# Stores of two gradient tiles moved from SyncE to ScalarE, and SyncE's order of transposing loads and late stores fixed by edges

## The chip, the cores and the metric

The kernel runs on one core of one Trainium2 chip. The metric is the device time of one execution in microseconds (us); before the change it is 480.02 us, the median of three runs (479.32 to 480.20). One further execution was taken with the hardware profiler; all durations below come from that one. Five engines work in parallel, each through its own instruction list in order: TensorE (PE, with its weight loads listed as PEld), VectorE (DVE), ScalarE (ACT), GpSimd (POOL) and SyncE (SP), which here does nothing but issue DMA transfers.

## The reference

A forward function and its gradients for a given `grad_out`, with S = 2048 positions, D = 512 channels and F = 1376 hidden units, all in bf16:

```python
def _A_ref(q, k, v, shift_k, ssm_k, ssm_D):
    ...
    for t in range(ks):                                  # a causal shift filter of 4 taps
        k_shift = k_shift + k_pad[:, t:t + S, :] * shift_k[:, ks - 1 - t][None, None, :]
    kv = k_shift * v
    ...
    y = irfft(rfft(kv) * rfft(ssm_k))[:S]                # a causal convolution over 2048 positions
    y = y + kv * ssm_D[None, None, :]
    return q * y
...
g = x @ w_gate; u = x @ w_up                             # x is the normalised A_q
B = (g * u) @ w_down
out = A_q + _A_ref(layernorm(A_q), ...) + B
_out, _vjp = jax.vjp(_f, A_q, A_k, A_v, A_shift_k, A_ssm_k, A_ssm_D, B_w_gate, B_w_up, B_w_down)
```

The outputs are `out` (out_0) and nine gradients: of A_q (out_1), A_k (out_2), A_v (out_3), the shift filter (out_4), ssm_k (out_5), ssm_D (out_6), w_gate (out_7), w_up (out_8) and w_down (out_9).

## The kernel before

The positions are split into 8 chunks of 256, F into 11 blocks `fb` (ten of 128 and a last one of 96). Up to about 316 us the kernel normalises, computes the gate and up projections and the hidden gradients chunk by chunk, and runs the forward and inverse transforms of the convolution in matrix form. Each chunk leaves a tile `hd` with three parts for each F block (the hidden product and the gradients of the two projections); seven of the eight chunks are stored to DRAM as `HDD`, the last one stays on chip.

The change lies in what follows, the part from `dw()` on. `dw()` runs over the 11 F blocks and does for each of them two products over all 16 rows of 128 positions:

- `down_grad(fb)` (L1022 to L1039): 16 matmuls `pd` of 512 columns, whose result ScalarE copies into `od` (two buffers) and SyncE stores into out_9 (L1034). For the last block the two halves of `od` are copied and stored by ScalarE and by VectorE with SyncE (L1036 to L1039).
- the products `pu` (L1062), 64 matmuls, whose result ScalarE copies into `og`; after every odd block, and after the last, SyncE stores `og` in two transfers into out_7 and out_8 (L1073). There is one `og` buffer, shared by two neighbouring blocks.

Both products need the block of the hidden tile with positions on the partitions, so it has to be transposed. For blocks 0 to 6 SyncE loads it as `hb` (L793, two buffers) and TensorE transposes it in `hid_t` (`pt`, L859), from where ScalarE copies it into `nath` and `natd`. For the last four blocks (`TURNED`, 7 to 10) `load_t` (L804 to L820) issues a transposing DMA on SyncE that writes `natT` directly: one load for blocks 7, 8 and 10, two for block 9, five in all. Block 7's takes the buffer of `hb` block 5, block 8's that of `hb` block 6, the others the buffers of earlier `natd` and `nath` tiles. The loads of block fb+2 are written in the middle of `down_grad(fb)`.

Four side generators are woven between the steps of `dw()`; the number n below counts the yields of `dw()`, six to a block:

- `inv_y` from n = 0, every 3rd step: the inverse transform; its VectorE products leave `kb`, stored by SyncE, and `dks`.
- `dsk_gram` from n = 27, every 2nd step: matmuls `pk` and VectorE's products `kd` (L1091) for the shift filter's gradient; TensorE's PSUM pool of three buffers (`p2`) is shared by `pk`, `pt`, `pu` and others.
- `inv_dk` from n = 35: the gradient of ssm_k (`po`, `o5t`).
- `ew` from n = 10, every 3rd step: VectorE's elementwise rounds. It runs the 16 pieces of `tail`: `final(b)` for b = 0 to 7 (out_0 and out_1, tiles `o` and `e`, two buffers each, which read a tile `bb` that `load_fin` loads one round ahead on SyncE, L1127) and `bwd(b)` (out_2, tile `dk`). Their results are put on the list `late`, and `put_late()` (L1178) issues the stores of one piece on SyncE ahead of the next piece.

The list of every engine is ordered when the program is built, by a planner of the framework that goes by its own estimates and by priorities: program order, which `tc.high_priority(offset=SOON)` raises by 300 places. `tc.issue_after(x)` adds an edge: what is traced in its block on the same engine as `x` stands behind `x` in that engine's list. It adds no wait, and nothing at all on another engine. `LG` holds the most recently traced instruction of a kind at the time that the code is traced. Before the change `behind(fb)` gives block 9's transposing loads an edge to the last `bb` load traced, and block 10's an edge to the last `og` store; blocks 7 and 8 have none. The numbering that follows from n: the stores of round 2 (`o`, `e`), `dk` 1 and the load of `bb` 4 are traced ahead of block 7's transposing load; `o`, `e` 3, `dk` 2 and `bb` 5 between block 7's and block 8's; `o`, `e` 4, `dk` 3 and `bb` 6 between block 8's and block 9's; `o`, `e` 5, `dk` 4 and `bb` 7 between block 9's and block 10's.

Of the kernel before, what the change touches and what calls it, by code (L numbers as in the profile page):

```python
# [24 lines left out]
NFB = len(FBLK)  # L25
# [165 lines left out]
def kernel(  # L191
# [24 lines left out]
    nc = tc.nc  # L216
# [14 lines left out]
    def cs(c):  # L231
        return slice(c * 128, (c + 1) * 128)

    def act(o, i):
        nc.scalar.copy(o, i)  # L235
# [7 lines left out]
    BX = dram.tile([P, R, 2, D], BF, name="BX")  # L243
# [8 lines left out]
    def P2(name, shape, dt=F32):  # L252
        return ps2.tile(shape, dt, name=name, tag="p2")

    def P1(name, shape, dt=F32):
        return ps1.tile(shape, dt, name=name, tag="p1")
# [399 lines left out]
    first = ExitStack()  # L656
# [131 lines left out]
    LG = {}  # L788

    def load_hb(fb):  # L790
        f0, fw = FBLK[fb]
        t = CP["b"].tile([P, NCH - 1, 3, 256], BF, name="hb")
        nc.sync.dma_start(t[:fw], HDD[:fw, fb])  # L793
        hbs[fb] = t
# [3 lines left out]
    TURNED = range(NFB - 4, NFB)  # L798

    def behind(fb):  # L800
        first = {NFB - 2: lambda: LG["bb"], NFB - 1: lambda: LG["og"]}.get(fb)
        return tc.issue_after(first().ins) if first else ExitStack()

    def load_t(fb):  # L804

        f0, fw = FBLK[fb]
        if fb == SPLIT:
            parts = ((0, 5, "n", dict(tag="natd", bufs=2)), (5, NCH - 1, "n", dict(tag="nath")))
        elif fw < P:
            parts = ((0, NCH - 1, "n", dict(tag="natd", bufs=2)),)  # L810
        else:
            parts = ((0, NCH - 1, "b", dict(tag="hb")),)
        nats[fb, 0] = {}
        for a, e, pool, kw in parts:
            t = CP[pool].tile([P, e - a, 3, 2, fw], BF, name="natT", **kw)
            with behind(fb) as _, tc.high_priority(offset=SOON):
                nc.sync.dma_start_transpose(out=t[:].rearrange("s c t h f -> s (c t h) f"),
                                            in_=HDD[:fw, fb, a:e].rearrange("p c t s -> p (c t s)"))
            for c in range(a, e):
                nats[fb, 0][c] = t[:, c - a]  # L820
# [3 lines left out]
    def last_t(fb):  # L824
        f0, fw = FBLK[fb]
        pt = P2("pt7", [P, 3, 2, P], BF)
        for t in range(3):
            for h in range(2):
                nc.tensor.transpose(pt[:, t, h, :fw], hds[1][:fw, fb, t, h * 128:h * 128 + 128], ident[:fw, :fw])
        n7 = c2b.tile([P, 3, 2, P], BF, name="nat7", tag="dd")  # L830
        act(n7[:, :, :, :fw], pt[:, :, :, :fw])
        nats[fb, 1] = n7

    def nat_h(fb, r):
        f0, fw = FBLK[fb]
        if fb not in TURNED:
            return nats[fb, 0][:, r, :fw]
        return nats[fb, 0][r // 2][:, 0, r % 2, :] if r < R - 2 else nats[fb, 1][:, 0, r % 2, :fw]

    def nat_d(fb, r):  # L840
        f0, fw = FBLK[fb]
        if fb not in TURNED:
            return nats[fb, 1][:, :, r, :fw]
        return nats[fb, 0][r // 2][:, 1:3, r % 2, :] if r < R - 2 else nats[fb, 1][:, 1:3, r % 2, :fw]

    def hid_t(fb, t):
        if fb in TURNED:
            return
        f0, fw = FBLK[fb]
        hb = hbs.pop(fb) if t == 2 else hbs[fb]  # L850
        if t == 0:
            nats[fb, 0] = CP["n"].tile([P, R, P], BF, name="nath")
        elif t == 1:
            nats[fb, 1] = CP["n"].tile([P, 2, R, P], BF, name="natd", bufs=2)
        dst = nats[fb, 0] if t == 0 else nats[fb, 1][:, t - 1]
        pt = P2("pt", [P, R, P], BF)
        for r in range(R):
            hs = hb[:fw, r // 2, t] if r < R - 2 else hds[1][:fw, fb, t]
            nc.tensor.transpose(pt[:, r, :fw], hs[:, (r % 2) * 128:(r % 2) * 128 + 128], ident[:fw, :fw])  # L859
        act(dst[:, :, :fw], pt[:, :, :fw])  # L860
# [161 lines left out]
    def down_grad(fb):  # L1022
        f0, fw = FBLK[fb]
        pd = P1("pd", [P, D])
        for r in range(R):
            nc.tensor.matmul(pd[:fw, :], lhsT=nat_h(fb, r), rhs=goC[:, r, :], start=(r == 0), stop=(r == R - 1))  # L1026
            if r == R // 2 - 1 and fb:
                hid_t(fb, 2)
                if fb + 2 < NFB:
                    load_h(fb + 2)  # L1030
        od = c2b.tile([P, D], BF, name="od")
        if fb + 1 < NFB:
            act(od[:fw], pd[:fw])
            nc.sync.dma_start(out_9[f0:f0 + fw, :], od[:fw])  # L1034
        else:
            for h, cp, q in ((0, act, nc.scalar), (1, dve, nc.sync)):  # L1036
                hc = slice(256 * h, 256 * h + 256)
                cp(od[:fw, hc], pd[:fw, hc])
                q.dma_start(out_9[f0:f0 + fw, hc], od[:fw, hc])  # L1039

    def load_h(fb):
        (load_t if fb in TURNED else load_hb)(fb)

    def dw():
        og = None
        load_hb(2)
        for fb, (f0, fw) in enumerate(FBLK):
            last = fb + 1 == NFB
            if not last:
                down_grad(fb)  # L1050
                yield
                hid_t(fb + 1, 0)
                hid_t(fb + 1, 1)
                yield
                yield
            pu = P2("pu", [P, NC4, 2, P])
            if fb % 2 == 0:
                og = c2b.tile([P, 2, NC4, P], BF, name="og1", tag="dd") if last else c2.tile([P, 2, NC4, 2 * P], BF, name="og")
            q0 = (fb % 2) * P
            for c in range(NC4):  # L1060
                for r in range(R):
                    nc.tensor.matmul(pu[:, c, :, :fw], lhsT=xnC[:, r, cs(c)], rhs=nat_d(fb, r),  # L1062
                                     start=(r == 0), stop=(r == R - 1))
                if c == 1:
                    yield
                    if fb + 1 in TURNED:
                        last_t(fb + 1)
                    yield
            act(og[:, :, :, q0:q0 + fw].rearrange("p t c f -> p c t f"), pu[:, :, :, :fw])
            if fb % 2 == 1 or last:  # L1070
                a = f0 - q0
                for t, o in enumerate((out_7, out_8)):
                    LG["og"] = nc.sync.dma_start(o[:, a:f0 + fw].rearrange("(c p) f -> p c f", p=128), og[:, t, :, :q0 + fw])  # L1073
            yield
            if last:
                down_grad(fb)
                yield
# [46 lines left out]

    def load_fin(b):
        bb = c2b.tile([P, 2, 2, D], BF, name="bb")
        LG["bb"] = nc.sync.dma_start(bb[:], BX[:, 2 * b:2 * b + 2, :, :])  # L1127
        FL[b] = bb

    def final(b):  # L1130
# [47 lines left out]
    def put_late():  # L1178
        for dst, t in late:
            nc.sync.dma_start(dst, t[:])  # L1180
        late.clear()

    def ew():
        with tc.issue_after(DKS[2].ins):
            load_fin(0)
        yield
        for f in tail:
            put_late()
            f()
            yield  # L1190
        with tc.issue_after(LG["og"].ins):
            put_late()
        yield

    def load_dk():
        gks.append(load_gk(0))
        gks.append(load_gk(1))
        yield

    sides = [every(seq(inv_y(), load_dk()), 0, 3), every(dsk_gram(), 27, 2), every(inv_dk(), 35, 3), every(ew(), 10, 3)]  # L1200
    for n, _ in enumerate(dw()):
        for sd in sides:
            if n >= sd[0]:
                sd[0] += sd[1]
                next(sd[2], None)
# [33 lines left out]
```

## Time and profile before

| What | Number |
|---|---|
| Median of three runs | 480.02 us |
| Profiled execution: its own time / span of its instructions | 481.82 / 480.0 us |
| Mean granted TensorE clock | 0.999 |
| TensorE without work, 312 to 400 us | 0.78 us |
| TensorE without work, 400 to 420 us | 1.32 us |
| TensorE without work, 420 to 475.8 us | 0.27 us |
| After TensorE's last matmul, to the end | 4.2 us |
| VectorE busy, 360 to 475.8 us | 97.7 of 115.8 us |
| ScalarE busy, 312 to 475.8 us | 78.0 of 163.8 us |
| `od` stores on SyncE | 10, median 0.454 us each (0.337 to 1.313) |
| `og` stores on SyncE | 12, median 0.722 us each (0.387 to 1.307) |
| `natT` transposing loads on SyncE | 5, 33.5 us together (2.6 to 9.7) |

The idle times of TensorE are the length of a window less its busy time there. An issue's duration is the time that the issuing engine spends on it; the data lands later. The letter q after an engine's name (SPq, ACTq) marks work of its instruction queue, issues among it. The figure in square brackets at the end of a timeline row is how long that engine had been idle before it, and what ended that.

### The profile page before, as it was taken

To read this page: it belongs to the slowest core of one execution; us is meant where nothing else is said; L and a number is where in the kernel's file an instruction comes from. 1 tells how busy PE (TensorE), PEld (TensorE's weight loads), DVE (VectorE), ACT (ScalarE), POOL (GpSimd) and SP (SyncE) were. 2 spreads that over 40 slices of the span, in tenths; PEclk is the share of its full clock that TensorE was granted. 3 is DMA by queue.
4 is the path that set the end of the run, shared out by engine and by line. 5 is a ranking of instruction groups with operands and counts; after the bars stand their busy time and mean duration, and the time that the engine had idled before them with its cause. 6 is when DMAs were issued, how large, how long until landed. Compare 5 with 4: busy or idle time off the path is not lost.

```text
span 480.0 us, 10366 instructions
## 1 busy us (share of the span) xinstructions
PE 464.5 (97%) x4252; PEld 311.6 (65%) x4293; DVE 340.5 (71%) x609; ACT 305.6 (64%) x349; POOL 14.0 (3%) x30
## 2 busy tenths in 40 slices
PE   7999999999999999999999999999999999999996
PEld 6867755547648447447447743576777687677885
DVE  7889989979366567686777877022257899599893
ACT  4957677659568678779779975375576535233141
POOL 8000000000000000000000000110000000000000
PEclk9999999999999999999999999999999999999999
DMA  8999999989998968968978379999899979999858
GB/s 268 374 381 366 310 296 320 315 300 328 318 288 270 277 202 255 285 200 245 298 235 259 118 272 331 388 329 313 312 361 364 371 260 320 318 267 239 252 155 294
DMA packets 111132, 139.85 MB, mean 291 GB/s; under 512 B 38859, under 2 KB 84336, under 8 KB 109550
## 3 DMA queue, kind: packets, MB, share of 16 engines
q1 hardware_dynamic: 109502, 137.85, 89.7%
q10 hardware_dynamic: 1584, 1.36, 1.0%
q8 instruction: 33, 0.54, 0.5%
q14 instruction: 13, 0.11, 0.1%
HBM read 67.08 MB, written 63.41 MB: 272 GB/s over the span
## 4 chain that ended last, share of the span: by engine, by line
PE 67%; DMA 15%; DVE 14%; issue 2%; SPq 2%; ACT 1%; DVEq 0%; ACTq 0%
PE px L555 15%; PE pgu L512 13%; PE pu L1062 8%; PE py L548 7%; PE pdh L518 6%; PE pd L1026 4%; PE ps L584 3%; DMA khC<-in_A_k_dram 3%; PE pg L613 3%; DMA ssk<-in_A_ssm_k_dram 2%; PE pf L370 2%; PE pt L859 2%; DMA vb<-in_A_v_dram 2%; DMA kb<-KS 2%; DMA x_b<-in_A_q_dram 2%
## 5 line engine op out<-in xcount | busy, mean ns | idle before, releaser
L555 PE MATMUL px<-WT,hd 128*128 128x512 bf16 (+1 forms) x340 | 78.6, 379 | 1.6 <-issue 1.4
L1062 PEld LDWEIGHTS <-xnC 128*128 128x128 bf16 x704 | 67.0, 98 | 8.4 <-issue 0.6
L555 PEld LDWEIGHTS <-hd 128*128 128x128 bf16 (+1 forms) x352 | 32.8, 98 | 44.4 <-issue 7.7
L235 ACT CAST gu<-pgu 128x1024 bf16<-128x1024 f32 (+1 forms) x48 | 45.4, 946 | 16.9 <-PE pgu L512 16.7
L235 ACT CAST GO<-pg 128x1024 bf16<-128x1024 f32 x48 | 46.2, 1015 | 13.8 <-issue 7.2
L235 ACT CAST SP<-ps 128x1024 bf16<-128x1024 f32 x47 | 45.5, 1025 | 13.7 <-PE ps L584 11.8
L512 PE MATMUL pgu<-xt,Wu 128*128 128x256 bf16 (+1 forms) x352 | 53.1, 273 | 1.1 <-DVE kn L238 0.6
L600 DVE TENSOR_TENSOR T<-SP 128x2048 bf16<-128x2048 bf16 x24 | 29.3, 1222 | 34.8 <-ACT SP L235 34.7
L512 PE MATMUL pgu<-xt,Wg 128*128 128x256 bf16 (+1 forms) x352 | 52.8, 273 | 0.0
L1062 PE MATMUL pu<-natd,xnC 128*128 128x256 bf16 x448 | 51.2, 273 | 0.0
L518 PE MATMUL pdh<-gt,WdT 128*128 128x256 bf16 (+1 forms) x352 | 46.9, 273 | 0.1
L235 ACT CAST fst<-pf 128x1024 bf16<-128x1024 f32 x44 | 42.7, 1031 | 5.5 <-issue 2.3
L512 PEld LDWEIGHTS <-Wu 128*128 128x128 bf16 (+1 forms) x352 | 33.0, 100 | 15.6 <-issue 10.7
L548 PE MATMUL py<-Wd,hd 128*128 128x512 bf16 (+1 forms) x167 | 40.2, 379 | 0.8 <-issue 0.5
L235 ACT CAST og<-pu 128x1024 bf16<-128x1024 f32 (+1 forms) x11 | 10.9, 993 | 43.7 <-PE pu L1062 28.3
L518 PEld LDWEIGHTS <-WdT 128*128 128x128 bf16 (+1 forms) x352 | 34.9, 100 | 4.8
L512 PEld LDWEIGHTS <-Wg 128*128 128x128 bf16 (+1 forms) x352 | 34.8, 100 | 3.7
L235 ACT COPY natd<-pt 128x2048 bf16<-128x2048 bf16 x14 | 26.2, 1875 | 12.0 <-PE pt L859 12.0
L533 DVE TENSOR_TENSOR hd<-gu,dh 128x1024 bf16<-128x1024 bf16 (+1 forms) x48 | 30.8, 641 | 0.8
L532 DVE TENSOR_TENSOR hd<-gu 128x512 bf16<-128x512 bf16 (+1 forms) x48 | 19.0, 397 | 16.7 <-ACT gu L235 16.7
L548 PEld LDWEIGHTS <-hd 128*128 128x128 bf16 (+1 forms) x176 | 16.5, 98 | 20.8 <-issue 3.1
L600 DVE TENSOR_TENSOR U<-SP 128x2048 bf16<-128x2048 bf16 x24 | 29.2, 1218 | 0.0
(177 smaller groups left out, 687.4 us busy)
## 6 DMA issues: line engine op xcount, KB each, us to landing
HDD<-hd SPq DMA_DIRECT2D x35, 384.0 KB, 4.5
FD<-fst SPq DMA_DIRECT2D x24, 512.0 KB, 4.9
X<-FD SPq DMA_DIRECT2D x24, 512.0 KB, 5.5
GD<-GO SPq DMA_DIRECT2D x24, 512.0 KB, 3.9
g<-GD SPq DMA_DIRECT2D x11, 1024.0 KB, 8.9
hb<-HDD SPq DMA_DIRECT2D x7, 1344.0 KB, 10.2
bb<-BX SPq DMA_DIRECT2D x8, 512.0 KB, 5.5
BX<-bx SPq DMA_DIRECT2D x7, 512.0 KB, 3.9
```

The lines of the kernel that those rows point to most:

```text
L235: nc.scalar.copy(o, i)
L512: nc.tensor.matmul(pgu[:w, i, t, :], lhsT=W[:, c, f0:f0 + w], rhs=xt[:, :, c, :], start=(c == 0), stop=(c == NC4 - 1))
L518: nc.tensor.matmul(pdh[:w, i, :], lhsT=WdT[:, c, f0:f0 + w], rhs=gt[:, :, c, :], start=(c == 0), stop=(c == NC4 - 1))
L532: nc.vector.tensor_tensor(hd[:fw, fb0:fb0 + n, 0, :], gu[:fw, :n, 0, :], gu[:fw, :n, 1, :], op=ALU.mult)
L533: nc.vector.tensor_tensor(hd[:fw, fb0:fb0 + n, 1:3, :], gu[:fw, :n], dh[:fw, :n].unsqueeze(2).to_broadcast((fw, n, 2, 256)), op=ALU.mult)
L548: nc.tensor.matmul(py[:], lhsT=hd[:fw, fb, 0, ss], rhs=Wd[:fw, fb, :], start=(fb == 0), stop=(fb == NFB - 1))
L555: nc.tensor.matmul(px[:], lhsT=hd[:fw, fb, t, ss], rhs=W[:fw, fb, :], start=(t == 1 and fb == 0), stop=(t == 2 and fb == NFB - 1))
L584: nc.tensor.matmul(ps[32 * q:32 * q + 32, a, :], lhsT=TB.EF[64 * a:64 * a + 64, 4 * g + q, ri].rearrange("p k j -> p (k j)"), rhs=X[64 * a ...
L600: tt(W[:].rearrange("p c a d -> p c (a d)"), A[:, i:i + 1].rearrange("p c a d -> p c (a d)").to_broadcast((P, 2, 2 * D)), B[:].rearrange(" ...
L613: nc.tensor.matmul(pg[q // 2][64 * a:64 * a + 64, q % 2, :], lhsT=TB.EI[32 * q:32 * q + 32, 2 * g + a, yi].rearrange("p k c -> p (k c)"), ...
L1026: nc.tensor.matmul(pd[:fw, :], lhsT=nat_h(fb, r), rhs=goC[:, r, :], start=(r == 0), stop=(r == R - 1))
L1062: nc.tensor.matmul(pu[:, c, :, :fw], lhsT=xnC[:, r, cs(c)], rhs=nat_d(fb, r), start=(r == 0), stop=(r == R - 1))
```

## The change

Four things change, all in this last part. The `od` stores of blocks 0 to 9 and all `og` stores are issued by ScalarE. `behind` gives the transposing loads of blocks 9 and 10 an edge to the last `bb` load traced. `LG["t"]` remembers the last transposing load traced, and `put_late()` gets an edge behind it, as does `load_fin(b)` for b > 4. The edge of the last `put_late()` to `LG["og"]` stays in the code; `og` is stored by ScalarE now, and the stores in that block are SyncE's, so that no edge comes of it.

```diff
     def behind(fb):
-        first = {NFB - 2: lambda: LG["bb"], NFB - 1: lambda: LG["og"]}.get(fb)
-        return tc.issue_after(first().ins) if first else ExitStack()
+        return tc.issue_after(LG["bb"].ins) if fb >= NFB - 2 else ExitStack()
...
-                nc.sync.dma_start_transpose(out=t[:].rearrange("s c t h f -> s (c t h) f"),
+                LG["t"] = nc.sync.dma_start_transpose(out=t[:].rearrange("s c t h f -> s (c t h) f"),
...
             act(od[:fw], pd[:fw])
-            nc.sync.dma_start(out_9[f0:f0 + fw, :], od[:fw])
+            nc.scalar.dma_start(out_9[f0:f0 + fw, :], od[:fw])
...
-                    LG["og"] = nc.sync.dma_start(o[:, a:f0 + fw].rearrange("(c p) f -> p c f", p=128), og[:, t, :, :q0 + fw])
+                    LG["og"] = nc.scalar.dma_start(o[:, a:f0 + fw].rearrange("(c p) f -> p c f", p=128), og[:, t, :, :q0 + fw])
...
     def load_fin(b):
         bb = c2b.tile([P, 2, 2, D], BF, name="bb")
-        LG["bb"] = nc.sync.dma_start(bb[:], BX[:, 2 * b:2 * b + 2, :, :])
+        with tc.issue_after(LG["t"].ins) if b > 4 else ExitStack():
+            LG["bb"] = nc.sync.dma_start(bb[:], BX[:, 2 * b:2 * b + 2, :, :])
...
         for f in tail:
-            put_late()
+            with tc.issue_after(LG["t"].ins) if "t" in LG else ExitStack():
+                put_late()
             f()
             yield
```

## The prediction

> **What bounds the kernel now.** I read the page first (engines, chain), then a table of windows over the last part, where every edited line lies, then who waits for whom, then the rows of SyncE, VectorE and TensorE around each wait.
>
> ```profile
> PE 464.5 (97%) x4252; PEld 311.6 (65%) x4293; DVE 340.5 (71%) x609; ACT 305.6 (64%) x349; POOL 14.0 (3%) x30
> ```
>
> ```profile
> 400.00:420.00 20.00, 18.68 (x210) 14.79 (x210) 14.27 (x29) 8.36 (x7) 0.00 (x0) 1.00 1.13 303
> 420.00:475.80 55.80, 55.53 (x525) 44.58 (x525) 49.06 (x90) 17.70 (x22) 0.00 (x0) 1.00 0.95 248
> 475.80:480.00 4.20, 0.04 (x1) 0.00 (x0) 0.42 (x1) 0.37 (x1) 0.00 (x0) 0.86 0.64 156
> ```
>
> The columns of the second view are window, length, then busy time of PE, PEld, DVE, ACT and POOL, clock and DMA. TensorE is without work for 0.27 us between 420 and 475.8 us, 1.32 us between 400 and 420, and 0.78 us from 312 to 400. So TensorE sets the time, and an edit that only moves transfers can win at most these gaps plus part of the last 4.2 us. The table of waits says who owns the largest gap, and the rows of the engines say how it comes about:
>
> ```profile
> PE pt L859 <- DVE kd L1091: 1.3, 2, 1.1
> ```
>
> ```profile
> 399.05 9.69 SPq L817 DMA_TRANSPOSE natT<-HDD  x1
> 408.79 0.57 SPq L1180 DMA_DIRECT2D out_dram<-o  x1
> ...
> 410.36 0.58 SPq L1127 DMA_DIRECT2D bb<-BX  x1
> 411.05 1.31 SPq L1034 DMA_DIRECT2D out_dram<-od  x1
> ...
> 419.32 0.75 SPq L1180 DMA_DIRECT2D out_dram<-o  x1
> 420.41 9.06 SPq L817 DMA_TRANSPOSE natT<-HDD  x1
> ...
> 433.80 10.00 SPq L817 DMA_TRANSPOSE natT<-HDD  x2
> ```
>
> ```profile
> 413.62 0.69 DVE L1138 TENSOR_TENSOR o<-xnC,yC 128x1024 bf16<-128x1024 bf16 x1 [4.29 <-DMA out_dram<-o]
> ...
> 416.00 0.69 DVE L1139 TENSOR_TENSOR o<-o,bb 128x1024 bf16<-128x1024 bf16 x1 [1.09 <-DMA bb<-BX]
> 416.72 0.86 DVE L1091 TENSOR_TENSOR kd<-pk,ident 64x256 f32<-64x256 f32 x2
> ...
> 426.52 0.68 DVE L1138 TENSOR_TENSOR o<-xnC,yC 128x1024 bf16<-128x1024 bf16 x1
> ```
>
> ```profile
> 417.64 0.95 PE L859 MATMUL pt<-ident,hb 128*128 128x128 bf16 x14 [1.06 <-DVE kd L1091]
> ```
>
> Read from the bottom: TensorE stands 1.06 us because VectorE's `kd` is late; `kd` is late because VectorE, in order, first waited 4.29 us for round 2's store of `o` (which frees the buffer of round 4's `o`) and 1.09 us for `bb` 4; both are late because SyncE spent 9.69 us issuing block 7's transposing load ahead of them. That round-2 `o` was computed by 381.1 us (its L1139 row starts at 380.42 and takes 0.69).
>
> **Part 1, the stores on ScalarE.** Ten `od` issues at 0.454 us (median of L1034) and twelve of `og` at 0.722 (L1073) leave SyncE: 4.5 + 8.7 = 13.2 us. ScalarE gets them; it is busy for 78.0 of the 163.8 us from 312 to 475.8, so there is room, but each issue stands between two of its copies. What follows `od` there:
>
> ```profile
> 400.93 0.59 ACT L235 CAST od<-pd 128x512 bf16<-128x512 f32 x1
> 401.84 1.87 ACT L235 COPY nath<-pt 128x2048 bf16<-128x2048 bf16 x1 [0.32 <-PE pt L859]
> ```
>
> The gap behind `od` is 0.24 to 0.32 us in the rounds up to 401 us. An issue of 0.34 (what `od` took at 317.8, 334.4, 351.0 and 371.1) pushes the next copy by some 0.1 us, one of 1.31 (the worst, at 411.05) by 1.0. Both `og` stores of a block, 2 x 0.722 = 1.44 us, fit before `natd` at 348.62 and 381.77 (1.6 us behind `og`'s cast). ScalarE has an idle stretch of 1.5 us or more in every block, so the push doesn't add up, and in the waits of TensorE from 312 us on no copy of ScalarE appears. TensorE's next user of a PSUM buffer starts 0.7 us or more after the copy that it could need: `pu` at 353.85 against the end of the `yC` copies at 353.14. I take 0; bounds: 0, and 1.0 - 0.7 = 0.3 us for each issue as long as the worst, of which ten would make 3 us. `og`'s buffer comes free earlier: its cast at 396.31 and at 456.22 had waited for the stores (13.0 us of idle time in two waits), but TensorE had no gap from it: 0.
>
> At the end ScalarE casts the last `og` by 473.28 and issues its two stores (0.87 and 1.15 us on SyncE) before its half of `od` at 475.88: 475.3, so 0.6 us of cover; at 1.31 each it would be 475.9, nothing lost. On SyncE the last `od` half follows its cast as before:
>
> ```profile
> 476.73 0.34 SPq L1039 DMA_DIRECT2D out_dram<-od  x1
> ```
>
> SyncE's closing wait for it, 1.1 us, is the last on a transfer, behind 0.3 for `dk` and 0.6 for `og`. The gap from this issue to the end of that wait is some 2.4 us, while quiet `od` stores land in 2.0. With `og` away earlier I take **0.3 us off**; bounds 0 and 0.4.
>
> **Part 2, the edges.** Three of them only confirm the old order: `o`, `e` 3, `dk` 2 and `bb` 5 stand behind block 7's load already (412.83 to 414.23), block 9's loads (433.80) directly behind `bb` 6 (433.34), and `o`, `e` 5, `dk` 4 and `bb` 7 behind those (444.48 to 446.33). Two move something. Block 10's load, now at 452.94 behind `og`, may go after `bb` 7 at 446.8; its first user is `pu` at 466.95, so it only gets earlier: 0. And round 4's `o`, at 419.32, must go behind block 8's load. That load can't start before TensorE's last read of `hb` block 6 at 418.9, takes 9.06, and so ends near 428.0; `o` is stored at 428 instead of 419.3, and VectorE's `o` of round 6, at 426.52, needs that store's landing (2.0 to 5.5 us by other store rows, so 430 to 433.5). If VectorE's list keeps this product where it is, VectorE is 3.5 to 7 us late; nothing of TensorE's waits for VectorE after 420 us until the end, where VectorE's last `dk` ends at 471.76 and its `od` cast starts at 476.28, a reserve of 4.5 us, and 1.68 us of VectorE's idle time at 445.3 absorbs more. I take 0; bounds 0 and 2.0 (7 less 4.5, and something less for the absorbed part).
>
> Not fixed by any edge is what costs the 1.06 us: block 7's load against round 2's `o`, `e`, `dk` 1 and `bb` 4. They are traced ahead of that load, which the raised priority puts first. I leave that as it is, 0; the other order is worth 1.06, and the 0.22 us gap at 401.96 (the other wait in the row of 1.3) has its `kd` before any of this and stays.
>
> **Sum.** 480.0 (span) + 0 - 0.3 + 0 + 0 = **479.7 us**. The profiled execution's span and the median of the runs, 480.02, are the same number within 0.1 us, so the sum needs no shift. Its own range, from the bounds that don't change the case: -0.4 to +0.6, 479.4 to 480.6.
>
> **Rivals.**
> (a) *Round 2 gets ahead.* With `og` and `od` gone from SyncE's list the planner may have issued `o` 2, `e` 2, `dk` 1 and `bb` 4 before block 7's load is due. They were ready at 381 to 395 us, and SyncE sits without an issue from 394.5 to 399.05, waiting for `hb` block 5's buffer; four issues of 0.5 us fit in. Then VectorE saves 4.29 + 1.09 us, `kd` comes some 5 us sooner and the gap closes: 480.0 - 1.06 - 0.3 = 478.6. Against it: the priority is unchanged, and it lost before.
> (b) *VectorE late to the end* (slower). As in part 2: the product for round 6's `o` stays in its place and its store's landing comes after 431 us. It decides from a delay of VectorE of 4.5 us at the end; at 6 us `od`'s last cast is 1.5 us late: 480.0 + 1.5 - 0.2 = 481.3. For it: the list has that product directly behind the old landing. Against it: the planner sees the new edge too, and may move the product down, and (a) would give VectorE 5.4 us back.
> (c) *ScalarE blocked behind SyncE's transposing loads* (slower). If one engine's issue excludes the other's for its whole length, the `od` store at 401.5 waits until 408.7, the `nath` copy starts 7.3 us late, and TensorE, with two of three PSUM buffers unread, stops at `pu` 404.83 until about 411: 6.2 us, 486. Against it: at the very start both engines issue at once, ScalarE at 0.72, 1.23 and 1.75 (0.48 to 0.53 us each) and SyncE at 0.73, 1.20 and 1.66 (0.41 to 0.43); six issues in 1.56 us, and 0.34 each in turn would be 2.0. That speaks against exclusion for the whole of a plain issue; no row has a ScalarE issue during a transposing one. [...]
>
> **How the numbers follow.** No change to speak of (479.7): 0.40; (a) 0.32; (b) 0.21; (c) 0.07. A measurement of this kernel tells some 0.2%, 0.96 us, from no change: faster means below 479.06, slower above 480.98. (a) is nearly all faster, and a little of the first case: 0.32. (c) and most of (b), with ScalarE's 3 us bound in a few hundredths: 0.28. The rest, 0.40, is within. The range must reach into (a) and most of (b), and leaves (c) out: 478.3 to 482.0.
>
> **What would show it.** Right: `od` and `og` issues among ScalarE's rows at 0.35 to 0.9 us, no ScalarE copy among TensorE's waits, SyncE's last wait on `od` near 0.8 us, and the wait of `pt` for `kd` still 1.06. (a) shows as `o` and `bb` rows ahead of the first `natT` row, and `pt` without that wait; (b) as an idle of VectorE of 4 us or more near 427, ended by the store of `o`, and an `od` cast later than the TensorE's end; (c) as ScalarE issues of several us. A new wait of TensorE for ScalarE above 0.5 us, or TensorE ending off 475.9 by more than 1 us, would make my sum wrong.

## The result and the profile after

| What | Before | After |
|---|---|---|
| Median, us (lowest to highest) | 480.02 (479.32 to 480.20) | 484.01 (482.89 to 484.30) |
| Ratio with 95% interval | | 1.0082 (1.0069 to 1.0096) |
| Profiled execution: own time / span, us | 481.82 / 480.0 | 484.22 / 482.4 |
| TensorE's last matmul ends, us | 475.84 | 479.04 |
| From there to the end of the span, us | 4.2 | 3.4 |

The change makes the kernel slower by 0.8%, outside the range that was given. The profile after is read in the order used for before: engines, windows, waits, then rows. The engines' totals are what they were; the loss isn't work:

```profile
PE 465.5 (96%) x4252; PEld 312.3 (65%) x4293; DVE 340.2 (71%) x609; ACT 305.8 (63%) x349; POOL 13.9 (3%) x30
```

The windows of after (same columns as before) put it into one place:

```profile
400.00:420.00 20.00, 16.45 (x188) 13.26 (x187) 19.12 (x37) 7.41 (x6) 0.00 (x0) 1.00 1.12 277
420.00:479.00 59.00, 57.82 (x546) 46.17 (x549) 44.03 (x82) 18.98 (x22) 0.00 (x0) 1.00 0.86 233
```

TensorE lacks 3.55 us between 400 and 420 (before 1.32) and 1.18 behind that (before 0.27), while VectorE is busy for 19.12 of those 20 us (before 14.27). VectorE has stopped waiting and does its work earlier, and TensorE waits more. The table of TensorE's waits in after names one owner, the same as before, with 4.5 us instead of 1.3:

```profile
PE pt L858 <- DVE kd L1090: 4.5, 2, 2.4
```

SyncE's rows of after show that the order of rival (a) did come about. The first two rows are round 2's `o` and `bb` 4 (`e` and `dk` 1 stand between them), ahead of block 7's transposing load; round 4's `o` stands behind block 8's load, as the edge asks:

```profile
392.10 0.92 SPq L1180 DMA_DIRECT2D out_dram<-o  x1
...
395.67 0.45 SPq L1127 DMA_DIRECT2D bb<-BX  x1
399.18 12.80 SPq L816 DMA_TRANSPOSE natT<-HDD  x1
...
422.00 5.36 SPq L816 DMA_TRANSPOSE natT<-HDD  x1
427.49 0.51 SPq L1180 DMA_DIRECT2D out_dram<-o  x1
```

So VectorE's waits for the store of `o` and for `bb`, 4.29 and 1.09 us before, shrink to 0.66 in this stretch. Yet `kd` comes later, not sooner. VectorE's rows of after say why:

```profile
400.50 1.00 DVE L1153 TENSOR_SCALAR e<-dxn,rstd,m 128x512 bf16<-128x512 f32 x2
401.53 0.69 DVE L1154 TENSOR_TENSOR e<-e,goC 128x1024 bf16<-128x1024 bf16 x1
402.14 1.22 DVE L1115 TENSOR_TENSOR tk<-dks,skb 128x2048 bf16<-128x2048 bf16 x1
403.39 0.86 DVE L1090 TENSOR_TENSOR kd<-pk,ident 64x256 f32<-64x256 f32 x2
...
416.00 0.69 DVE L1138 TENSOR_TENSOR o<-xnC,yC 128x1024 bf16<-128x1024 bf16 x1 [0.66 <-DMA out_dram<-o]
...
418.26 1.22 DVE L1115 TENSOR_TENSOR tk<-dks,skb 128x2048 bf16<-128x2048 bf16 x1
419.40 0.69 DVE L1139 TENSOR_TENSOR o<-o,bb 128x1024 bf16<-128x1024 bf16 x1
420.10 0.86 DVE L1090 TENSOR_TENSOR kd<-pk,ident 64x256 f32<-64x256 f32 x2
```

Almost no brackets: VectorE isn't waiting, it is doing other things first. The list itself has another order. `kd` runs in four pairs, called kd 1 to kd 4 here. These are VectorE's rows of before around kd 2:

```profile
400.49 0.54 DVE L1153 TENSOR_SCALAR e<-dxn,rstd,m 128x512 bf16<-128x512 f32 x1
401.05 0.86 DVE L1091 TENSOR_TENSOR kd<-pk,ident 64x256 f32<-64x256 f32 x2
401.94 0.55 DVE L1153 TENSOR_SCALAR e<-dxn,rstd,m 128x512 bf16<-128x512 f32 x1
402.40 0.42 DVE L1093 TENSOR_REDUCE dsk<-kd 128x4 f32<-128x256 f32 x1
402.73 0.68 DVE L1154 TENSOR_TENSOR e<-e,goC 128x1024 bf16<-128x1024 bf16 x1
```

Before, kd 2 stood between the two L1153 products of `e` and ran at 401.05; now it stands behind both, behind L1154 and behind the first `tk` product of the next piece: 403.39. kd 4 ran at 416.72 even behind its two waits; now it runs at 420.10, behind the rest of a round, the `o` and `e` products of the next round, a `tk` and an `o` sum. Its input `pk` had been done since 412.7. TensorE's own list has the same order as before. Its rows show the price:

```profile
404.30 0.96 PE L858 MATMUL pt<-ident,hb 128*128 128x128 bf16 x14 [2.42 <-DVE kd L1090]
...
421.02 0.95 PE L858 MATMUL pt<-ident,hb 128*128 128x128 bf16 x14 [2.09 <-DVE kd L1090]
```

The second of these rows had 1.06 us in its bracket before; the first was:

```profile
401.96 0.96 PE L859 MATMUL pt<-ident,hb 128*128 128x128 bf16 x14 [0.22 <-DVE kd L1091]
```

2.42 + 2.09 = 4.5 us, 3.2 more than the 1.3 before, and TensorE ends 3.2 us later. With the shorter tail 2.4 us are left between the two spans, less than the medians' 3.99; the first run of the next section says why.

### The profile page after: what moved, and what is told of

The parts are those of the page before. It is cut to its first block, busy times and chain, and to the rows that moved or that the text cites. A ratio compares the mean times of both kernels' runs of the same rounds, so it can differ in the third digit from the quotient of the medians.

```text
span 482.4 us, 10356 instructions
## 1 busy us (share of the span) xinstructions
PE 465.5 (96%) x4252; PEld 312.3 (65%) x4293; DVE 340.2 (71%) x609; ACT 305.8 (63%) x349; POOL 13.9 (3%) x30
## 4 chain that ended last, share of the span: by engine, by line
PE 62%; DVE 10%; DMA 7%; issue 2%; ACT 1%; SPq 1%; DVEq 0%; ACTq 0%
PE pgu L512 12%; PE px L555 11%; PE pu L1061 11%; PE py L548 6%; PE pdh L518 6%; PE pd L1025 5%; PE ps L584 3%; PE pg L613 3%; PE pt L858 2%; DMA bb<-BX 2%; DMA out_dram<-kb 2%; PE pq L931 2%; PE po L1000 1%; DMA FD<-fst 1%; SPq L816 1%
```

## The experiments

Theory: VectorE's new order, `kd` behind elementwise rounds, costs all of the loss; ScalarE's issues and SyncE's new order cost nothing. Rivals: the issues on ScalarE cost the time, or the later stores of `o` do, or the transposing loads in their new places. Line numbers of the diffs are left out; the `kd` edges need `LG["kd"] = ` ahead of L1091's operation.

**The kernel before, again.** No edit.

> The kernel before, unchanged, as a control and for a second profile of it. Ratio 1.000 (0.998 to 1.002). Every theory expects the same. The profile also tells whether the 1.06 us wait of the transposes for kd is there in every execution: in the first profile of before the span was 480.0 us while its own time was 1.8 us above the median of the runs, so an ordinary execution may have a span near 478.2 us; if the gap at kd is what varies, this profile shows it near 0 with a span near 478.9.

480.35 us, ratio 0.9999 (0.9983 to 1.0015), span 478.6. Its window from 400 to 420 us, and then the only row of TensorE's waits behind 300 us:

```profile
400.00:420.00 20.00, 20.00 (x230) 15.99 (x229) 15.11 (x33) 9.98 (x8) 0.00 (x0) 1.00 1.12 314
```

```profile
PE ptd L1017 <- DVE dskt L238: 0.6, 1, 0.6
```

No wait for `kd` at all: the wait that the prediction was built around isn't there in every execution of the unchanged kernel. TensorE ends at 475.25 and the tail is 3.35 us, as in after. Against this execution after's span is 3.8 us longer, and its TensorE ends 3.79 us later: 4.5 us of waits for `kd` less the 0.6 here. That is close to the medians' difference of 3.99.

**The two parts by themselves.**

```diff
-            nc.sync.dma_start(out_9[f0:f0 + fw, :], od[:fw])
+            nc.scalar.dma_start(out_9[f0:f0 + fw, :], od[:fw])
...
-                    LG["og"] = nc.sync.dma_start(...)
+                    LG["og"] = nc.scalar.dma_start(...)
```

> od and og stores on ScalarE, edges as before (the one of block 10's load behind og falls away, as og is no longer SyncE's). In its list VectorE has the second and the fourth pair of kd behind as much of the rounds' work as in the changed kernel. Theory 1 (VectorE's list makes kd late): the transposes wait for kd 4 to 5 us, as in the changed kernel (4.5), and the time is 1.006 to 1.010 of before. Theory 2 (the new edges put stores behind the long transposing loads, which starves VectorE): without the edges the loss is gone, 0.998 to 1.002.

The stores alone: 485.87 us, ratio 1.0142 (1.0098 to 1.0187), span 482.6, waits for `kd` 3.8 us, for `dskt` 0.5 and for `natd` 0.2. The loss is there without the edges, which speaks against theory 2; but the time lies above theory 1's range. One of the six executions took 492.13 us; the other five average 1.011 of before.

The edges alone (the change with both stores given back to SyncE):

> The edges of the change, with od and og stores left on SyncE. VectorE's list keeps all four pairs of kd where before has them. Theory 1: the waits for kd stay near 1.3 us and the time near before, 0.998 to 1.003; round 4's o waits behind block 8's load, so VectorE idles some us near 427, which reaches no matmul. Theory 2: the loss is here, 1.006 to 1.010.

480.02 us, ratio 1.0000 (0.9982 to 1.0018), waits for `kd` 0.9 us. All four pairs of `kd` have their places of before in VectorE's list. Behind them the list has changed: the product of round 6's `o`, which needs the store that the edge delays, stands further down (at 433.75 instead of 426.52), and the idle time expected near 427 didn't come. So the loss comes with the stores' move, and the edges by themselves do nothing that can be measured.

**VectorE's order put back, with everything else of the change left in.** An edge on VectorE holds an elementwise piece behind the `kd` traced before it; it adds no wait. First for piece 7, `final(4)`, alone:

```diff
-        for f in tail:
+        for m, f in enumerate(tail):
...
-            f()
+            with tc.issue_after(LG["kd"].ins) if m in (7,) else ExitStack():
+                f()
```

> The changed kernel with one more edge: final(4)'s VectorE instructions stand behind the last kd traced, so that the third and fourth pairs come ahead of round 4; the second pair stays where the change has it. Theory 1: of the two waits of the transposes for kd (2.42 at 404 us and 2.09 at 421) the first stays, the second goes: the sum falls from 4.5 to 2.4 (2.2 to 2.9), and the time by some 2.1 us, to 1.004 of before (1.002 to 1.006). Theory 2: nothing changes for SyncE's transposing loads, so 1.007 to 1.010 stays.

The second wait is gone and the first stays (2.43 us), as expected. The time is above the expected range: 483.19 us, 1.0066 (1.0040 to 1.0092), only 0.8 us below the change. The windows of this profile show what took the rest in this execution. TensorE stands still behind 401.8, starts again at 404.22, and then the granted clock (third number from the end) falls:

```profile
404.00:406.00 2.00, 1.78 (x24) 1.49 (x26) 1.97 (x4) 0.56 (x1) 0.00 (x0) 0.76 1.83 273
406.00:408.00 2.00, 2.00 (x22) 1.69 (x20) 1.73 (x3) 1.30 (x1) 0.00 (x0) 0.50 0.56 111
408.00:410.00 2.00, 2.00 (x22) 1.61 (x19) 1.14 (x3) 0.00 (x0) 0.00 (x0) 0.89 1.22 142
```

2 x (0.24 + 0.50 + 0.11) = 1.7 us of clock lost, an estimate from these three windows, against 2.09 won. The 32 `pk` matmuls that start at 405.33 took 3.43 us here and 1.94 us in after. The median isn't explained by it: the three of the seven executions with a mean clock of 1.00 took 481.89, 483.12 and 483.46 us, about as long as the four with 0.996 (482.63 to 486.11). What kept those three long stays open. Then for every piece:

```diff
+            with tc.issue_after(LG["kd"].ins) if "kd" in LG else ExitStack():
+                f()
```

> The changed kernel with VectorE's rounds behind the kd pairs traced ahead of them, all four: od and og stay with ScalarE, SyncE's edges stay. Theory 1: the transposes' waits for kd (4.5 us in the changed kernel, 2.4 with the fourth pair alone put ahead) fall under 0.5 us, and the time to that of before: 0.996 to 1.002, 478 to 481 us. Rival (ScalarE's 22 issues or SyncE's new order cost something of their own): the waits for kd go, and a rest of the loss stays, 1.003 to 1.006.

480.19 us, 0.9993 (0.9970 to 1.0015): the whole loss is gone, with ScalarE issuing all 22 stores and every edge of SyncE's in place. TensorE's and ScalarE's lists in this last part have the order that they have in after, and SyncE's too but for a few stores of `dk` and `o` a few places off; so it is VectorE's order that was put back. No wait for `kd` is left, and TensorE's window is full again:

```profile
400.00:420.00 20.00, 19.95 (x230) 16.08 (x230) 17.43 (x36) 9.83 (x8) 0.00 (x0) 1.00 1.12 313
```

An edge for pieces 6 and 7 puts kd 2 one `tk` product (1.22 us) earlier and kd 4 first:

> As the run with the fourth pair first, and the second pair of kd also one instruction up in VectorE's list, ahead of bwd(2)'s first tk (1.22 us). Theory 1: the one wait at pt falls from 2.4 to 1.2 us (1.0 to 1.4), the time by as much, to 1.002 to 1.005. If the wait for kd were a symptom of something else that is late, one instruction more or less ahead of it would leave the wait at 2.4 and the time at 1.0066.

480.40 us, 1.0018 (0.9994 to 1.0043); one wait, 1.43 us. Both lie just outside their expected ranges, and the interval reaches below 1, so what is left of the wait isn't told apart in the time. The wait shrinks by 1.0 from 2.43, and the median by 2.8 from the run with the edge for piece 7. The wait followed the place of kd 2 to within 0.3 us. The time fell by more than the wait. None of the 12 executions here has a mean granted clock below 0.998, and four of seven there had 0.996; but by the times above the clock accounts at most for a part of that.

**The same edges on the kernel before.**

> The kernel before with the same edges for kd, and nothing of the change. Theory 1: before loses 0 to 1.3 us to kd (1.3 in its first profile, 0 in its second), so the gain is at most that: 0.996 to 1.001. If VectorE, held at a kd that TensorE has not fed yet, now waits itself, its rounds come later by 1 to 3 us, which has 4.5 us of cover at the end.

480.02 us, 0.9987 (0.9971 to 1.0003), no wait for `kd`.

> The kernel before with the fourth pair alone put ahead of round 4's instructions (the first three stay where they are). Theory 1: the second of before's two waits (1.06 us in one profile, 0.7 in that of the edges alone, 0 in the control's) can't come up, the first (0.2) can: 0.997 to 1.000, the least gap of all the kernels at pt.

479.43 us, 0.9987 (0.9971 to 1.0003), no wait for `kd`, span 477.6. It is the lowest median of all kernels here, but both intervals reach past 1, so neither is shown to beat the kernel before. That fits with a kernel whose wait for `kd` is 1.3 us in one execution and none in another.

**Is it SyncE's order that moves VectorE's?** The kernel before, stores on SyncE, with block 7's load put behind `bb` 4, which brings round 2 ahead:

```diff
-        first = {NFB - 2: lambda: LG["bb"], NFB - 1: lambda: LG["og"]}.get(fb)
+        first = {NFB - 4: lambda: LG["bb"], NFB - 2: lambda: LG["bb"], NFB - 1: lambda: LG["og"]}.get(fb)
```

> The kernel before with one edge: block 7's transposing load behind bb 4, so that round 2's o, e, dk 1 and bb 4 go ahead of it in SyncE's list, as they do in the changed kernel; od and og stay with SyncE. In VectorE's list the second pair of kd stays as in before, the fourth falls behind most of round 4. Theory 1 (it is the order in which SyncE's stores let VectorE's rounds run ahead that pushes kd back, whoever stores od and og): one wait at pt near 420 us of 1.5 to 3.5 us, none above 0.5 near 402; 1.002 to 1.007. Rival (the stores on ScalarE are needed for the loss): no wait above 1.1, 0.997 to 1.001, as VectorE saves the 5.4 us that it stood for o and bb.

480.18 us, 0.9995 (0.9979 to 1.0012), no wait for `kd`; kd 2 at 400.23, kd 4 at 414.86. The first theory of that text missed in the wait, not in the order. Round 2 ahead of the load does put kd 4 behind most of round 4 in VectorE's list, while kd 2 keeps its place:

```profile
407.08 0.68 DVE L1138 TENSOR_TENSOR o<-xnC,yC 128x1024 bf16<-128x1024 bf16 x1
...
409.61 0.68 DVE L1139 TENSOR_TENSOR o<-o,bb 128x1024 bf16<-128x1024 bf16 x1
...
412.98 1.41 DVE L1152 SCALAR_TENSOR_TENSOR dxn<-xnC,m,dxn 128x512 f32<-128x512 bf16 x2
414.31 0.54 DVE L1153 TENSOR_SCALAR e<-dxn,rstd,m 128x512 bf16<-128x512 f32 x1
414.86 0.86 DVE L1091 TENSOR_TENSOR kd<-pk,ident 64x256 f32<-64x256 f32 x2
```

But VectorE no longer stands still for `o` and `bb`, so kd 4 still runs 1.9 us earlier than in before, where it ran at 416.72, and no wait comes of it. kd 4's later place in the list cost no time here, since the product still came in time for TensorE. This is rival (a)'s order made by hand, and it wins nothing that can be measured either.

**One store each.** Only `od` on ScalarE:

> Only the ten od stores on ScalarE, nothing else of the change. VectorE's list has the second pair of kd behind all of round 3's final, but ahead of bwd(2), and the fourth behind three more instructions of round 4 than before; SyncE issues round 2's o ahead of block 7's load, its e, dk and bb 4 behind it. Theory 1: wait at the first pt of 1.2 us (2.42 less one tk of 1.22), at the second of 0.9 to 1.8; together 2.1 to 3.0, time 1.003 to 1.006. Rival (the loss grows with the issues that ScalarE gets, 4.5 of 13.2 us): 1.002 to 1.004 with no wait for kd above 0.5.

482.93 us, 1.0067 (1.0042 to 1.0092), a little above the expected range, with two waits for `kd`, 1.20 and 1.64 us, both as expected. TensorE's row of the first:

```profile
402.35 0.96 PE L859 MATMUL pt<-ident,hb 128*128 128x128 bf16 x14 [1.20 <-DVE kd L1091]
```

Only `og` on ScalarE:

> Only the twelve og stores on ScalarE. VectorE's list has the second pair of kd one tk further down, as in the changed kernel, the fourth behind four scalar_tensor_tensor of round 4 and round 5's o. Theory 1: first wait 2.4 us, second 0.9 to 2.0, together 3.3 to 4.4, time 1.006 to 1.010. Rival (ScalarE's issues, 8.7 of 13.2 us): no wait for kd above 0.5.

485.69 us, 1.0122 (1.0080 to 1.0163). Here the expectation missed: one wait for `kd` (1.87 us), but also 2.23 us for the load of `hb` at 386.5 and 0.89 for a `nat` copy of ScalarE at 450.7; 5.0 us in these three, and behind the load's wait the clock at 0.57 from 386 to 390. With `og` alone moved there are other waits than with both moved, so the two halves don't add up to the whole. Why the load and the copy are late here was not followed up.

**The stores alone, once more**, in one execution, because they came out slower than the whole change:

> The stores alone once more, for a second profile: its median (485.9) lay 1.5 us above the one profiled execution (484.4) and 1.9 above the changed kernel. The waits for kd explain 3.8 us in that profile. If the rest is a wait that the new edges keep away, this profile shows it behind 420 us: block 9's loads stand directly behind block 8's and ahead of the load of g for po, and dk 4 and bb 7 behind block 10's.

486.03 us; waits for `kd` 0.45 + 2.56 + 1.36 us, for an `o5t` copy 0.6 and for `dskt` 0.5, 5.5 in all. That is 1.0 us more than after's 4.5 us of waits for `kd`, where the span is 1.8 us longer; the rest of it is open. Four of the six executions of the first run had a mean clock of 0.996 or less, against one of five of the change, which would be another part. What in the edges holds those waits off was not separated.

## Why the prediction failed

**The step that failed** is in rival (a) and in the last paragraph of Part 2: "VectorE saves 4.29 + 1.09 us, `kd` comes some 5 us sooner and the gap closes", and "the 0.22 us gap at 401.96 ... has its `kd` before any of this and stays". Both hold VectorE's list fixed and only slide it in time. VectorE did get 4.7 us of its waits back, but with 22 issues gone from SyncE's list the planner had also ordered VectorE's anew, and kd 2 and kd 4 stood behind elementwise products that they had stood ahead of. The gap of 0.22 us grew to 2.42 and that of 1.06 to 2.09. In the terms of the sum, it is the last 0, for the two waits for `kd` that were to stay as they are (1.3 us together): it measured 3.2 us. Putting `kd` first by hand gives all of it back (1.0082 to 0.9993); that is what shows the cause. Why the planner chose so isn't in any trace. The sum had no term for such a new order, and the range's upper end no case: rival (b) said itself that the planner may move the product of round 6's `o`, but the same thought wasn't turned on `kd`, the one VectorE product that TensorE waits for in the profile of before.

**The base.** "The profiled execution's span and the median of the runs ... are the same number within 0.1 us, so the sum needs no shift" compared unlike things. The span must be set beside the own time less what lies around the span: 481.82 is 1.8 us above its span of 480.0, as in every run here, so that execution was 1.8 above the median. The unchanged kernel's second execution, 1.4 us shorter, lacks the 1.3 us of waits. So rival (a)'s prize of 1.06 us was not there in every run to be won, and round 2 put ahead by hand, which brings that order without the loss, measured 0.9995. The lower end of the sum's own range is a slip as well: 480.0 less 0.4 is 479.6, not 479.4.

**Part 1, ScalarE: right.** Ten `od` issues took 0.345 to 0.363 us and twelve of `og` 0.378 to 0.957, with medians of 0.352 and 0.410 against SyncE's 0.454 and 0.722; no ScalarE copy is among TensorE's waits in after, and the run with `kd` first keeps all of them at no loss. Single ScalarE copies do appear among TensorE's waits with the stores alone (0.2 us in one profile, 0.6 in the other) and with `og` alone (0.89); whether the issues delay them isn't shown. One reading of the prediction was wrong: the row at 353.85, taken for TensorE's `pu`, is VectorE's; `pu` starts at 353.66, 0.52 us behind the `yC` copies and not 0.7. With issues of 0.36 us at most behind `od` nothing came of it.

**The tail: not shown.** I took 0.3 us off; it is 0.8 shorter here. But the unchanged kernel's second execution also has 3.35 us, and the runs with edges on `kd` lie between 3.3 and 4.1, so the profile of before had a long one, and neither size is told apart from that scatter. SyncE's last wait on `od` is still 1.1 us, where I said 0.8.

**Part 2, the edges: right in SyncE's moves and in the price of 0.** Block 10's load goes earlier, to 448.98, and the edges alone give 1.0000. Round 4's `o` is issued at 427.49, where I had said 428; that this agrees is luck. Block 8's load started at 422.00, not at 418.9, since the transposes that had waited for kd 4 read `hb` block 6 until then, and it took 5.36 us, not 9.06.

**Rival (b): no.** The late store did not reach the end. The planner moved the product of round 6's `o` down, as the argument against this rival had it: in before it ran at 426.52, ahead of the `dk` products around it; in after it starts at 435.68, behind them, without a wait. VectorE idles 4.71 us at 441.7 for `bb` and only 1.65 at 449.3 for `o`, and had been done for 7.6 us when its last `od` cast began at 479.48.

**Rival (c): no.** One of ScalarE's rows of after, inside SyncE's 12.80 us issue that began at 399.18:

```profile
401.68 0.35 ACTq L1033 DMA_DIRECT2D out_dram<-od  x1
```

0.35 us, where exclusion for the whole issue would have given 10.3 (to 411.98). The `od` issues at 424.50 and 453.47 lie inside SyncE's issues of blocks 8 and 10 (5.36 us from 422.00, 7.37 from 448.98) and took 0.35 each as well. No run shows the exclusion that this rival's 6.2 us is worked out from.

## What to carry to other kernels

Where a planner orders each engine's list, a DMA moved to another engine can change any list; here VectorE's changed, which the edit doesn't touch, and TensorE's didn't. Ask which product the bottleneck engine waits for, and whether something else may now be put ahead of it; an order edge on that product keeps the edit to what it says. And before pricing a wait from one profiled execution, set that execution's own time beside the median: a wait of the size of their difference may not be there to win.

## What the hardware showed that I had not expected

**The granted clock fell behind two of the waits.** The fall to 0.50 (406 to 408 us) behind the 2.43 us wait above, estimated there at 1.7 us, and the clock of 0.57 from 386 to 390 behind the 2.23 us wait of the run with `og` alone, are not in any table of waits. It doesn't follow every time: in after's own profile the clock stays at 1.00 behind 2.42 and 2.09 us. A mean granted clock of 0.997 or less is found in none of 94 executions of the kernel before, in one of five of the change, four of seven with the edge for piece 7, four of six with the stores alone, three of twelve with `od` alone and one of six with `og` alone. But it is also found in two of twelve with every `kd` first and in one of twelve of the kernel before with the same edges, whose profiled executions have no such wait. So what starts it isn't settled. Nor is its price: with every `kd` first the two are the slowest, at 483.12 and 483.32 against 478.80 to 480.80 for the others; with the edge for piece 7 the low clock didn't set the executions apart.

**Transposing loads of the same size took SyncE very different times to issue.** The loads of blocks 7 and 8 move 42 blocks of 128x128 each; in the profile of after they took 12.80 us at 399.18 and 5.36 at 422.00, in that of before 9.69 and 9.06. SyncE's next issue, a store each time, began 0.05 to 0.13 us behind the load's end: at 412.03 and 427.49 in after, at 408.79 and 429.56 in before.
